# A fixed order for all five engines through attention, and the last batch's rows mixed with the first expert block

## The chip, the cores and the metric

The kernel runs on one core of a Trainium2 chip. The core has five engines that run at the same time and wait for one another through semaphores: PE (TensorE: matmuls, and transposes written as matmuls), DVE (VectorE), ACT (ScalarE), POOL (GpSimd) and SP (SyncE, which here only issues DMAs). The metric is the device time of one execution in microseconds; lower is better. The median of three runs of the kernel before is 874.22 us (874.01 to 875.73).

## The reference

Three stages follow one another. The first is attention with a decay bias over 4 batches and 8 heads of 576 positions of width 64; the second sends each of the 2304 rows of width 512 to one of 8 experts; the third is a dense feed-forward with a cosine.

```python
scores = scale * np.matmul(q, k.transpose(0, 1, 3, 2))
cum = np.cumsum(np.maximum(s, 0.0), axis=-1)
bias = -(cum[:, :, :, None] - cum[:, :, None, :])
scores = np.where(causal, -1e9, scores + np.minimum(bias, 0.0))
attn = np.exp(scores - np.max(scores, axis=-1, keepdims=True))
x = np.matmul(attn / (attn.sum(-1, keepdims=True) + 1e-09), v)   # rows of 512: 8 heads x 64
xn = x / (np.linalg.norm(x, axis=-1, keepdims=True) + 1e-06)
logits = xn @ en.T / tau                      # 8 experts
expert_idx = np.argmax(logits, axis=1)        # one expert each
out[mask] = gate_w[mask, None] * (np.maximum(x[mask] @ w1[e], 0.0) @ w2[e])
h = x @ w_in                                  # 2304 x 2048
y = (h * np.cos(h)) @ w_out
```

The norm of a row, its eight logits and its gate (the softmax value of the chosen expert) all need the finished row of attention, with all eight heads.

## The kernel before

**Attention** runs over 16 pairs of heads, four pairs for each batch. Of a pair, the scores of four groups of query tiles are made on PE (`s_ps`, `emit_s`), the decay bias is added and the row's extreme taken on DVE (L299), the exponential is on ACT (L565), PE turns the result around with 64-wide transposes into `t_ps` (L315), DVE and ACT copy these into `pt` and `pu` (L574, L571), and PE multiplies them with the values into `o_ps` (`av`, L340), which ACT and DVE copy into the batch's output `ot` (L645, L610). The loop runs this as a pipeline: in the turn of pair p stand the transposes and value products of pair p and the scores of pair p+1. In the trace the matmul `o_ps<-pt,v_t` with 320 columns comes once in each pair, so the distance between two of them is the time of one pair.

The decay bias of a pair comes from a tile `c_t`: SP loads it from a running sum that was written to memory at the start (`cumd`, L107, L109), and POOL adds the causal mask to it (`mask`, L129 to L134). `c_t`, q and k have two buffers each and are issued two pairs ahead, v has three. By the page a pair loads 320 KB of q, 496 KB of k, 320 KB of v and 800 KB of `c_t` (one DMA of 512 KB, two of 144), 1.98 MB in all. The zero fill of the expert buffer `xr` (eight DMAs of 768 KB, L250) is issued four at a time between the loads of two pairs.

**Rows.** When a batch's four pairs are done, a generator `rows(b)` is drawn forward a step at marked points of the loop (`point`). It makes the unnormalised logits with eight matmuls (`lp_ps`, L383), turns them (`lt_ps`, L404), turns the rows (`r_ps`, L361), scales them on DVE (L368), squares and sums them on ACT (L377), chooses the expert on DVE (L418 to L458), counts positions on PE (`rk_ps`), takes the square root of the squared norm with POOL's power and four DVE steps (`root`, L208 to L215), makes the gate, multiplies the rows with it (POOL L505 for the first three batches) and scatters them into `xr` (POOL L510). Logits, their transposes and the ranks use the two buffers of the score tile `s`. `rows(0)` does its first real work in pair 5; the rows of batch 2 therefore end after the loop, and those of batch 3 stand wholly behind it.

**Hand-over.** The largest expert after three batches is chosen (`pick_first`); 256 of its rows are loaded back from `xr` and turned (`early_rows`, `xe_ps` L549) into `the` and `tle`. The expert stage `moe1` walks through steps (r, f): r = -1 is the early block (256 rows, eight weight chunks), r = 0 is the rest of the same expert (128 rows), then seven more experts. A step is 12 matmuls `h_ps` (L867 to L869) and, one step later, 12 matmuls `acc` (L900 to L902), because each product is made of three parts (`wh`, `wl` are the upper and lower part of a weight chunk, split on ACT L802 and DVE L804). r = 0 starts with `xt_ps` (L835), the turned late rows, which need the scatter of the last batch.

Attention's SP, PE, ACT and DVE stand in program order; POOL there, and all but SP in `moe1`, are ordered by the framework's scheduler.

Of the kernel before, what the change touches and what calls it, by code (L numbers as in the profile page):

```python
# [41 lines left out]
@with_exitstack  # L42
def moe_kernel(ctx, tc, qd, kd, vd, sd, ied, embt, tau, ident, maskd, trid, wcat, wf, out):
    nc = tc.nc
    const = ctx.enter_context(tc.tile_pool(name="const", bufs=1))
    dram = ctx.enter_context(tc.tile_pool(name="dram", bufs=1, space=DRAM))
    xr = dram.tile([E * NT, DM], F32, name="xr")
    count = ctx.enter_context(tc.tile_pool(name="count", bufs=1))

    g = G()  # L50
    g.count = count
    early = ExitStack()
    ep = early.enter_context(tc.tile_pool(name="early", bufs=1, side="right"))
    g.the = ep.tile([128, 4, EARLY], F32R, name="the")
    g.tle = ep.tile([128, 4, EARLY], F32R, name="tle")
    g.tc, g.nc, g.const, g.dram, g.xr, g.out = tc, nc, const, dram, xr, out
    ET = mybir.EngineType
    with tc.manual_schedule(engines={ET.SP, ET.PE, ET.Activation, ET.DVE}):
        attention(g, qd, kd, vd, sd, ied, embt, tau, ident, maskd, trid)
    with tc.manual_schedule(engines={mybir.EngineType.SP}):  # L60
        st = ctx.enter_context(ExitStack())
        g.rawp = st.enter_context(tc.tile_pool(name="rawp", bufs=3, reuse_waits="tile"))
        g.ringp = st.enter_context(tc.tile_pool(name="ringp", bufs=RING, reuse_waits="tile"))
        g.x2p = st.enter_context(tc.tile_pool(name="x2p", bufs=1, reuse_waits="tile"))
        g.cv = st.enter_context(tc.tile_pool(name="cv", bufs=1, reuse_waits="tile"))
        g.chunks, g.tasks, g.loading = {}, [], {}
        moe1(g, wcat, wf)
# [11 lines left out]
def attention(g, qd, kd, vd, sd, ied, embt, tau, ident, maskd, trid):  # L79
    tc, nc, const, dram, xr = g.tc, g.nc, g.const, g.dram, g.xr  # L80
    with ExitStack() as st:
        ld = st.enter_context(tc.tile_pool(name="a_ld", bufs=2))
        one = st.enter_context(tc.tile_pool(name="a_one", bufs=1))
        sx = st.enter_context(tc.tile_pool(name="a_sx", bufs=8))
        otp = st.enter_context(tc.tile_pool(name="a_ot", bufs=2))
        sm = st.enter_context(tc.tile_pool(name="a_sm", bufs=4))
        xp = st.enter_context(tc.tile_pool(name="a_x", bufs=7))
        ps_s = st.enter_context(tc.tile_pool(name="ps_s", bufs=2, space=PSUM))
        ps_t = st.enter_context(tc.tile_pool(name="ps_t", bufs=4, space=PSUM))

        qt, kt, ct, vt = {}, {}, {}, {}
# [12 lines left out]
        def load_c(p):  # L104

            c_t = ct[p] = ld.tile([128, CT], F32, tag="c", name="c_t")
            nc.sync.dma_start(out=heads(c_t)[:, :, 128:640], in_=cumd[2 * p:2 * p + 2, 0:512].unsqueeze(0).to_broadcast([128, 2, 512]))  # L107
            for h in range(2):
                nc.sync.dma_start(out=c_t[64 * h:64 * h + 64, 2 * CH:CT], in_=cumd[2 * p + h].unsqueeze(0).to_broadcast([64, S]))  # L109

# [14 lines left out]
        def mask(p):  # L125

            c = heads(ct[p])
            tail = ct[p][:, CT - 64:CT]
            nc.gpsimd.tensor_tensor(out=tail, in0=tail, in1=mk_f[:, 128:192], op=ALU.add)  # L129
            mk = mk_f[:, 0:128].unsqueeze(1).to_broadcast([128, 2, 128])  # L130
# [5 lines left out]

        def load_v(p):
            vt[p] = ld.tile([128, 5, 128], F32, tag="v", name="v_t", bufs=3)
            nc.sync.dma_start(out=vt[p], in_=vd[p])
# [16 lines left out]
        ct[0] = ld.tile([128, CT], F32, tag="c", name="c_t")  # L156
# [3 lines left out]
        def first_c(k):  # L160
            sel = sel2 if k == 2 else idt[0:B * H, k:k + 1].to_broadcast([B * H, 128])
            for c0, eng in ((0, nc.scalar.copy), (288, nc.vector.tensor_copy)):
                ps = ps_t.tile([128, 512], F32, tag="t", name="c_ps")[:, 0:288]
# [4 lines left out]

        load(1)
        load_v(0)  # L170
        load_c(1)
        load_v(1)
        ie = one.tile([128, 256], F32, name="ie")
        lgs = one.tile([128, 640], F32, name="lgs")
# [7 lines left out]
        half5 = one.tile([128, 8], F32, name="half5")  # L182
# [7 lines left out]
        cacc = one.tile([128, E], BF16, name="cacc")  # L190
# [4 lines left out]
        prev = []  # L195

        def unordered(ins):

            for o in prev:
                tc.declare_no_dep(ins.ins, o, reason="rows that differ")  # L200
            prev.append(ins.ins)

        def root(out_t, in_t, w):

            a = sm.tile([128, 8], F32, tag="ra", name="ra", bufs=2)
            c = sm.tile([128, 8], F32, tag="rb", name="rb", bufs=2)
            y = sm.tile([128, 8], F32, tag="rc", name="rc", bufs=2)
            nc.vector.tensor_scalar(out=a[:, 0:w], in0=in_t, scalar1=1e-30, scalar2=None, op0=ALU.add)  # L208
            nc.gpsimd.tensor_tensor(out=y[:, 0:w], in0=a[:, 0:w], in1=half5[:, 0:w], op=ALU.pow)
            for _ in range(2):  # L210
                yield
            nc.vector.reciprocal(out=c[:, 0:w], in_=y[:, 0:w])
            nc.vector.tensor_tensor(out=c[:, 0:w], in0=c[:, 0:w], in1=a[:, 0:w], op=ALU.mult)
            nc.vector.tensor_tensor(out=c[:, 0:w], in0=c[:, 0:w], in1=y[:, 0:w], op=ALU.add)
            nc.vector.tensor_scalar(out=out_t, in0=c[:, 0:w], scalar1=0.5, scalar2=1e-6, op0=ALU.mult, op1=ALU.add)  # L215

        def setup():
# [4 lines left out]
            nc.gpsimd.memset(zr, 0.0)  # L222
            nc.gpsimd.memset(lgs[:, S:640], 0.0)
            nc.vector.memset(ones_f, 1.0)
            nc.vector.memset(half5, 0.5)
            nc.vector.memset(ones_b, 1.0)
            nc.vector.memset(cacc, 0.0)
            yield

            nc.gpsimd.iota(ei, pattern=[[1, E]], base=0, channel_multiplier=0)  # L230
            nc.vector.tensor_copy(out=ef, in_=ei)
            nc.vector.tensor_scalar(out=rev, in0=ef, scalar1=-1.0, scalar2=float(E), op0=ALU.mult, op1=ALU.add)
            nc.vector.tensor_scalar(out=eb, in0=ef, scalar1=float(NT), scalar2=None, op0=ALU.mult)
            for _ in range(8):
                yield
            nc.vector.tensor_copy(out=tri_b, in_=tri_f)
            nc.vector.tensor_tensor(out=sq, in0=emb_t, in1=emb_t, op=ALU.mult)
            yield
            yield "a"
            np_ = ps_s.tile([128, 2, 512], F32, tag="s", name="n_ps")[:, 0, 0:E]  # L240
            for kk in range(4):
                nc.tensor.matmul(out=np_, lhsT=ones_f, rhs=sq[:, kk, :], start=(kk == 0), stop=(kk == 3))
            yield "ra"
            yield from root(en, np_, E)
            nc.vector.tensor_scalar(out=en, in0=en, scalar1=tau_t, scalar2=None, op0=ALU.mult)
            nc.vector.reciprocal(out=ien, in_=en)
            for e in range(E):
                for _ in range(2):
                    yield
                nc.sync.dma_start(out=xr[e * NT:e * NT + 384].rearrange("(p c) d -> p c d", p=128), in_=zr.unsqueeze(1).to_broadcast([128, 3, DM]))  # L250

# [27 lines left out]
        def emit_x(n):  # L279
            p, tiles = steps[n]  # L280
            b, hp = divmod(p, H // 2)
            if b not in rs:
                rs[b] = sm.tile([128, 5, H], F32, tag="rs", name="rs", bufs=2)
                nc.gpsimd.memset(rs[b][:, 4, :], 1.0)
# [3 lines left out]
            for h in (2,) if tiles == (4,) else range(2):  # L288
                t = sx.tile([128, S], F32, tag="sx", name="s_sb")
                px[n].append(t)  # L290
                for i, (q0, q1), o in places(tiles):
                    mx = sm.tile([128, 1], F32, tag="mx", name="mx", bufs=20)
# [11 lines left out]
        def emit_t(n):  # L304
# [3 lines left out]
            tps = [ps_t.tile([128, 512], F32, tag="t", name="t_ps") for u in range(2)]  # L308
# [20 lines left out]
        def av(p, c0):  # L329
# [5 lines left out]
            o = ps_t.tile([128, 512], F32, tag="t", name="o_ps")  # L335
# [8 lines left out]
        def rows(b):  # L344
            s3 = [128, 5, E]
            o = ot.pop(b)
            ri = sm.tile([128, 5, H], F32, tag="ri", name="ri", bufs=2)
            ss = sm.tile([128, 5], F32, tag="ss", name="ss", bufs=2)
            l = small(s3, "l")
            order = list(range(5))[::-1] if b == B - 1 else list(range(5))  # L350
            xs, rr = {}, {}
            pick = choose(b, l)

            def turn(n):
                i = order[n]
                q0, q1 = QT[i]
                rr[i] = [ps_t.tile([128, 512], F32, tag="t", name="r_ps") for h in range(2)]
                for e in range(4):
                    for h in range(2):
                        hs = slice(64 * h, 64 * h + 64)  # L360
                        nc.tensor.transpose(rr[i][h][0:q1 - q0, 64 * e:64 * e + 64], o[hs, e, q0:q1], idt[hs, hs])  # L361

            def scaled(n):
                i = order[n]
                m = QT[i][1] - QT[i][0]
                x = xs[i] = xp.tile([128, DM], F32, tag="x", name="x")
                for h, r in enumerate(rr.pop(i)):
                    nc.vector.tensor_tensor(  # L368
                        out=x[0:m].rearrange("p (e c) -> p e c", e=4)[:, :, 64 * h:64 * h + 64],
# [854 lines left out]
```

## Time and profile before

| what | value |
|---|---|
| median of 3 runs | 874.22 us |
| profiled execution: its own time | 872.18 us |
| its span, first to last instruction | 870.4 us |
| PE busy | 810.1 us, 93% |
| DVE busy | 579.0 us, 67% |
| ACT busy | 428.1 us, 49% |
| POOL busy | 129.6 us, 15% |
| mean granted TensorE clock | 0.972 |

The page cuts the span into 40 equal slices and writes the busy share of each in tenths:

```profile
PE   7887989855999999999999999999999999999994
DVE  5765989846456565656589968775777748544462
PEclk9999999975999999999999999999999999999998
```

One digit is 21.8 us. A share of busy time mixes stages: here PE is full from slice 11 to the last but one, and has its holes in the first ten slices, which hold attention and the hand-over to the experts. The granted clock (last line) falls in slices 9 and 10.

### The profile page before, as it was taken

The numbers are of one execution on the slowest core, as the hardware profiler recorded it, in microseconds if no ns is written. First come the engines' busy times: TensorE is split into PE (matmuls) and PEld (weight loads), VectorE is DVE, ScalarE is ACT, GpSimd is POOL, SyncE is SP. The second block draws the span as 40 slices with busy tenths as digits, with TensorE's granted clock in tenths as the row PEclk, the third lists the DMA queues.
The fourth block names the chain that finished last, engine by engine and source line by source line (L and its number), as shares of the span: only waits on it lengthen the run. The fifth ranks groups of instructions, "written<-read, shape, count | busy, mean of one in ns | idle before, by whom it ended". The sixth has DMA issues, their size and how long they took to land. (4 is left out here: it accounts for less than half of the span.)

```text
span 870.4 us, 14996 instructions
## 1 busy us (share of the span) xinstructions
PE 810.1 (93%) x5534; PEld 672.2 (77%) x5534; DVE 579.0 (67%) x1323; ACT 428.1 (49%) x916; POOL 129.6 (15%) x183
## 2 busy tenths in 40 slices
PE   7887989855999999999999999999999999999994
PEld 3555656534999999999998888888888888888883
DVE  5765989846456565656589968775777748544462
ACT  4776878824354454555537545343444434333331
POOL 3413474542100111111000000000000000000132
PEclk9999999975999999999999999999999999999998
DMA  6997676305976767887543212110111100000122
GB/s 209 282 377 222 209 240 208 109 36 188 328 265 150 145 151 170 173 173 151 167 156 86 95 49 73 49 49 25 49 49 49 50 0 1 1 1 0 49 85 87
DMA packets 41228, 107.84 MB, mean 124 GB/s; under 512 B 7486, under 2 KB 7998, under 8 KB 41150
## 3 DMA queue, kind: packets, MB, share of 16 engines
q1 hardware_dynamic: 37550, 97.30, 38.9%
q0 software_dynamic: 3552, 9.45, 2.9%
q8 instruction: 45, 0.74, 0.4%
q14 instruction: 33, 0.27, 0.1%
q10 hardware_dynamic: 48, 0.07, 0.0%
HBM read 91.00 MB, written 15.81 MB: 123 GB/s over the span
## 5 line engine op out<-in xcount | busy, mean ns | idle before, releaser
L804 DVE TENSOR_TENSOR wl<-wraw,wh 128x1024 fp32r<-128x1024 f32 x64 | 78.4, 1225 | 76.7 <-ACT wh L802 71.4
L1120 PE MATMUL h_ps<-x2h,wh 128*128 128x512 f32 (+1 forms) x320 | 118.4, 371 | 0.0
L1122 PE MATMUL h_ps<-x2h,wl 128*128 128x512 f32 (+1 forms) x320 | 118.3, 370 | 0.0
L1121 PE MATMUL h_ps<-x2l,wh 128*128 128x512 f32 (+1 forms) x320 | 118.1, 370 | 0.0
L1140 PE MATMUL facc<-wh,gh 128*128 128x512 f32 x288 | 114.9, 399 | 1.3 <-ACT gh L1127 1.3
L1142 PE MATMUL facc<-wh,gl 128*128 128x512 f32 x288 | 113.8, 396 | 0.0
L1141 PE MATMUL facc<-wl,gh 128*128 128x512 f32 x288 | 113.8, 395 | 0.0
L981 ACT ACTIVATE ki<-h_ps 128x512 int32<-128x512 f32 (+1 forms) x80 | 44.6, 557 | 119.6 <-PE h_ps L1122 115.0
L982 DVE SCALAR_TENSOR_TENSOR ki<-ki,h_ps 128x512 f32<-128x512 int32 (+1 forms) x80 | 50.5, 632 | 71.3 <-ACT ki L981 68.2
L802 ACT CAST wh<-wraw 128x1024 fp32r<-128x1024 f32 x64 | 67.1, 1049 | 51.2 <-PE acc L901 44.3
L565 ACT ACTIVATE s_sb<-s_sb,mx 128x576 f32<-128x576 f32 (+2 forms) x144 | 82.8, 579 | 11.0 <-DVE mx L299 10.8
L1152 POOL DMA_INDIRECT out_dram<-oacc,ti x18 | 17.5, 971 | 435.0 <-DVE oacc L1150 431.4
L901 PE MATMUL acc<-hl,wh 128*128 128x256 f32 (+7 forms) x256 | 76.7, 301 | 0.9 <-DVE hl L873 0.8
L983 ACT ACTIVATE ki<-ki,hpi 128x512 f32<-128x512 f32 (+1 forms) x80 | 54.5, 682 | 46.9 <-DVE ki L982 46.2
L902 PE MATMUL acc<-hh,wl 128*128 128x256 f32 (+7 forms) x256 | 76.5, 300 | 0.0
L900 PE MATMUL acc<-hh,wh 128*128 128x256 f32 (+7 forms) x256 | 76.3, 304 | 0.0
L1127 ACT CAST gh<-ki 128x512 fp32r<-128x512 f32 (+1 forms) x80 | 46.2, 578 | 51.6 <-DVE ki L984 51.1
L1121 PEld LDWEIGHTS h_ps<-x2l,wh 128*128 128x128 f32 x320 | 60.1, 188 | 12.5 <-DVE x2l L908 0.6
L1120 PEld LDWEIGHTS h_ps<-x2h,wh 128*128 128x128 f32 x320 | 60.0, 188 | 12.2
L1122 PEld LDWEIGHTS h_ps<-x2h,wl 128*128 128x128 f32 x320 | 60.1, 188 | 11.1
L299 DVE CUSTOM_DVE_ANT_0 s_sb<-s_ps,c_t 128x512 f32<-128x512 f32 (+3 forms) x112 | 58.3, 542 | 15.3 <-POOL c_t L129 12.8
L867 PE MATMUL h_ps<-xth,wh 128*128 128x368 f32 (+6 forms) x224 | 68.2, 304 | 0.0
(220 smaller groups left out, 1709.4 us busy)
## 6 DMA issues: line engine op xcount, KB each, us to landing
wraw<-in_wcat_dram SPq DMA_DIRECT2D x64, 512.0 KB, 4.9
wraw<-in_wf_dram SPq DMA_DIRECT2D x32, 512.0 KB, 3.6
k_t<-in_kd_dram SPq DMA_DIRECT2D x16, 496.0 KB, 4.9
c_t<-cumd SPq DMA_DIRECT2D x15, 512.0 KB
xr<-zr SPq DMA_DIRECT2D x8, 768.0 KB, 11.3
q_t<-in_qd_dram SPq DMA_DIRECT2D x16, 320.0 KB
v_t<-in_vd_dram SPq DMA_DIRECT2D x16, 320.0 KB, 6.1
c_t<-cumd SPq DMA_DIRECT2D x30, 144.0 KB, 4.7
```

What stands on the lines that cost most here:

```text
L565: nc.scalar.activation(**kw)
L804: nc.vector.tensor_tensor(out=lo, in0=raw, in1=hi.bitcast(F32), op=ALU.subtract)
L867: nc.tensor.matmul(out=ps[:, 0:c], lhsT=wh[:, sl], rhs=th[:, k, 0:c], start=(k == 0), stop=False)
L900: nc.tensor.matmul(out=ps[:, 0:c], lhsT=wh[:, sl], rhs=hh[:, 0:c], start=(f == 0), stop=False)
L901: nc.tensor.matmul(out=ps[:, 0:c], lhsT=wh[:, sl], rhs=hl[:, 0:c], start=False, stop=False)
L902: nc.tensor.matmul(out=ps[:, 0:c], lhsT=wl[:, sl], rhs=hh[:, 0:c], start=False, stop=(f == 7))
L1120: nc.tensor.matmul(out=ps[:, 0:w], lhsT=wh[:, sl], rhs=g.x2h[:, k, a0:a1], start=(k == 0), stop=False)
L1121: nc.tensor.matmul(out=ps[:, 0:w], lhsT=wh[:, sl], rhs=g.x2l[:, k, a0:a1], start=False, stop=False)
L1122: nc.tensor.matmul(out=ps[:, 0:w], lhsT=wl[:, sl], rhs=g.x2h[:, k, a0:a1], start=False, stop=(k == 3))
L1140: nc.tensor.matmul(out=acc[t], lhsT=gh[:, sl], rhs=wh[:, 512:1024], start=(c == s), stop=False)
L1141: nc.tensor.matmul(out=acc[t], lhsT=gh[:, sl], rhs=wl[:, 512:1024], start=False, stop=False)
L1142: nc.tensor.matmul(out=acc[t], lhsT=gl[:, sl], rhs=wh[:, 512:1024], start=False, stop=(c == e))
```

## The change

Attention, the rows and the first seven steps of the expert stage are now one list, written out for all five engines, POOL included.

- **Rows** become a class whose steps are entered in a table of pair and place (`at(p, where, ...)`). Batch b starts in pair 4b+4, one pair earlier than before. The four outputs of a batch are squared on ACT as they finish (`squares`), and eight more matmuls of `lp` add up these squares, so that norm and logits come out of the same transposes. The square root is eight steps on POOL; for the first three batches the sum over heads and the positions also run on POOL. The rows are turned with full 128-wide transposes after the gate is known and are scaled once, by gate over sum (`rg`), straight out of PSUM.
- **Loads.** `c_t` has three buffers and is loaded three pairs ahead and masked earlier, v has two buffers, and the zero fill is spread over pairs 0 to 5. At the start `c_t` of pair 1 is loaded ahead of q, k and v.
- **Hand-over.** The first weight chunks are loaded in pair 14 and split in pair 15. `overlap` puts the rows of batch 3 between the steps of the early block.
- Pools are laid out anew, so that the weight buffers exist during attention; `lp`, `lt`, `rk` use the four buffers of the tile `t`.

```diff
+            for e0, src in enumerate((o, sqo)):
+                for k, ps in enumerate(self.p):
+                    for e in range(4):
+                        w = 256 if e0 else 128 + 32 * e
+                        nc.tensor.matmul(out=ps[32 * e:32 * e + 32, 0:288], lhsT=ie[:, w:w + 32], rhs=src[:, e, 288 * k:288 * k + 288],
+                                         start=not e0, stop=bool(e0))
...
-            c_t = ct[p] = ld.tile([128, CT], F32, tag="c", name="c_t")
+            c_t = ct[p] = ld.tile([128, CT], F32, tag="c", name="c_t", bufs=3)
...
+            at(p, "a", r.lp)
+            at(p, "ra", r.lcopy)
+            at(p, "b", r.lt)
+            at(p + 1, "rb", r.lw, r.choose, r.norm)
+            at(p + 1, "x0", r.choice)
+            at(p + 1, "a", r.rank)
+            at(p + 1, "ra", r.gate_a)
+            at(p + 1, "x3", r.gate_b, r.place)
+            at(p + 1, "b", r.gate_c)
...
+        at(15, "x0", early_load)
...
+        squares(NPAIR - 1)
+        r = g.r = Rows(B - 1)
+        r.lp()
+        r.lcopy()
+        early_rows()
+        r.lt()
+        r.lw()
+        r.choose()
+        r.choice()
+        r.norm()
...
+    h(0)
+    split_(3)
+    weigh(6)
+    h(1)
+    r.rank()
+    o(0)
+    r.gate_a()
+    r.gate_b()
+    r.place()
+    r.gate_c()
+    split_(4)
+    weigh(7)
+    h(2)
+    r.turn(4)
+    r.turn(3)
+    o(1)
+    r.scaled(4)
+    r.scaled(3)
...
+    r.turn(0)
+    o(4)
+    r.scaled(0)
+    s.raw32(9)
+    counts()
+    h(6)
+    o(5)
+    s.raw32(10)
+    s.x(0)
+    s.x(1)
```

PE from the last value product on, before: the whole chain of batch 3 (`lp`, `lt`, `r_ps`, `rk`) stands ahead of `xe_ps` and of the first expert matmul.

```order
L340 MATMUL o_ps<-pu,v_t 64x128 x2
...
L383 MATMUL lp_ps<-ot,ie 32x288 x8
L385 MATMUL lp_ps<-rs,ie 128x4
L361 MATMUL r_ps<-idt,ot 64x64 x8
L361 MATMUL r_ps<-idt,ot 128x64 x8
L404 MATMUL lt_ps<-idt,lgs 128x64 x10
L361 MATMUL r_ps<-idt,ot 128x64 x24
...
L549 MATMUL xe_ps<-idt,x 128x128 x8
...
L867 MATMUL h_ps<-the,wh 128x256
```

The same stretch of PE now, down to the first turned rows of batch 3:

```order
L379 MATMUL o_ps<-pu,v_t 64x128 x2
L407 MATMUL lp_ps<-ot,ie 32x288 x8
L407 MATMUL lp_ps<-sqo,ie 32x288 x8
L409 MATMUL lp_ps<-rs,ie 128x4
L574 MATMUL xe_ps<-idt,x 128x128 x8
L425 MATMUL lt_ps<-idt,lgs 128x64 x10
L936 MATMUL h_ps<-the,wh 128x256
...
L468 MATMUL rk_ps<-oh_all,tri_b 128x40
...
L515 MATMUL r_ps<-idt,ot 64x128 x4
L515 MATMUL r_ps<-idt,ot 128x128 x4
```

Moved: 24 matmuls `h_ps` stand between `lt` and the ranks, 12 `acc` and 12 `h_ps` between the ranks and the turned rows.

DMA queue of SP at the start, before (behind the loads of pair 0):

```order
L101 DMA q_t<-in_qd_dram 128x640
L102 DMA k_t<-in_kd_dram 128x992
L139 DMA v_t<-in_vd_dram 128x640
L107 DMA c_t<-cumd 128x2x512
L109 DMA c_t<-cumd 64x576 x2
```

The same place now, to the second `c_t`:

```order
L139 DMA c_t<-cumd 128x2x512
L141 DMA c_t<-cumd 64x576 x2
L133 DMA q_t<-in_qd_dram 128x640
L134 DMA k_t<-in_kd_dram 128x992
L145 DMA v_t<-in_vd_dram 128x640
L251 DMA ie<-in_ied_dram 128x288
```

The loads of pair 1 now stand behind `c_t`, which waits until the running sum has landed in memory.

POOL for the rows of a batch before, between two masks: one power, then multiplications and scatters.

```order
L209 TENSOR_TENSOR rc<-ra,half_138 128x5
L392 MEMSET ss 64x1
L131 TENSOR_TENSOR c_t<-c_t,mk_f 128x2x128
...
L505 TENSOR_TENSOR x<-x,gt 128x512 x2
L510 DMA xr<-x,pi 18432x512 x2
```

POOL for the rows of a batch now, as far as the power of the norm (the rest of the norm and the positions follow):

```order
L440 TENSOR_TENSOR lw<-lw,ri 128x40
L445 TENSOR_TENSOR lw<-lw 128x5x36
L445 TENSOR_TENSOR lw<-lw 128x5x18
L445 TENSOR_TENSOR lg<-lw 128x45
L446 TENSOR_TENSOR l<-lg,ien 128x40
L265 TENSOR_SCALAR ra<-lg 128x5
L266 TENSOR_TENSOR rz<-ra,half_142 128x5
```

The multiplications of whole rows have left POOL, and 13 small steps for the choice and the norm, then nine for the positions, have come to it.

## Rows read from the trace of the kernel before

**Rows 1.** Stretches: start:end, us, busy PE, PEld, DVE, ACT, POOL, PEclk, DMA share, GB/s
```profile
22.64:34.02 11.38, 9.01 (x112) 6.06 (x110) 7.96 (x30) 9.24 (x30) 3.89 (x7) 1.00 0.97 257
...
43.55:51.35 7.80, 7.68 (x104) 5.03 (x102) 6.48 (x26) 7.16 (x24) 0.00 (x0) 1.00 1.03 372
...
63.51:79.36 15.85, 11.14 (x130) 6.97 (x129) 6.75 (x24) 8.48 (x26) 5.44 (x9) 0.89 0.86 248
...
106.61:118.91 12.30, 9.78 (x130) 6.48 (x128) 9.85 (x37) 8.46 (x28) 10.03 (x13) 1.00 0.76 239
...
181.30:208.84 27.54, 9.19 (x87) 6.04 (x85) 12.44 (x53) 7.09 (x17) 12.36 (x12) 0.59 0.34 117
208.84:236.65 27.81, 26.59 (x193) 25.75 (x193) 17.77 (x50) 12.16 (x21) 5.31 (x6) 0.85 0.81 287
```

**Rows 2.** PE in order of time, hand-over: start, us, instruction, [idle before <-releaser]
```profile
180.54 0.82 PE L340 MATMUL o_ps<-pu,v_t 128*64 128x256 f32 x8
...
186.72 0.80 PE L404 MATMUL lt_ps<-idt,lgs 64*128 64x64 f32 x10 [2.79 <-ACT lgs L388]
...
202.91 0.45 PE L549 MATMUL xe_ps<-idt,x 128*128 128x128 f32 x1 [2.51 <-DMA x<-xr]
...
208.84 0.58 PE L867 MATMUL h_ps<-the,wh 128*128 128x256 f32 x1 [1.90 <-ACT wh L802]
...
237.98 2.05 PE L858 MATMUL h_ps<-x,w 128*128 128x128 f32 x16 [0.68 <-ACT x L836]
```

**Rows 3.** PE in order of time, two and two matmuls of the early block
```profile
211.90 0.42 PE L867 MATMUL h_ps<-the,wh 128*128 128x256 f32 x1
...
213.19 0.41 PE L867 MATMUL h_ps<-the,wh 128*128 128x256 f32 x1
...
217.87 0.28 PE L867 MATMUL h_ps<-the,wh 128*128 128x256 f32 x1
...
220.71 0.28 PE L867 MATMUL h_ps<-the,wh 128*128 128x256 f32 x1
```

**Rows 4.** Stretches of 1 us, for the granted clock
```profile
187.00:188.00 1.00, 0.52 (x10) 0.33 (x7) 0.47 (x2) 0.00 (x0) 1.00 (x2) 0.50 0.00 0
...
217.00:218.00 1.00, 1.00 (x11) 1.00 (x10) 1.00 (x2) 0.55 (x1) 0.88 (x1) 0.98 0.98 401
```

**Rows 5.** Waits, 22 to 64 us: who, for whom, us in total, times, longest
```profile
DVE s_sb L299 <- POOL c_t L129: 6.4, 2, 4.0
DVE rb L212 <- POOL rc L209: 2.5, 1, 2.5
...
POOL c_t L131 <- DMA c_t<-cumd: 26.2, 4, 13.2
```

**Rows 6.** Waits, 64 to 119 us
```profile
PE lp_ps L383 <- DVE mx L299: 1.5, 1, 1.5
...
DVE s_sb L299 <- POOL c_t L129: 6.0, 1, 6.0
```

**Rows 7.** Instructions in order of time, durations of single kinds (PE, DVE, ACT)
```profile
77.64 1.18 PE L383 MATMUL lp_ps<-ot,ie 128*32 128x288 f32 x16
...
236.65 0.66 PE L835 MATMUL xt_ps<-idt,xw 128*128 128x128 f32 x4
...
165.62 0.78 ACT L565 ACTIVATE s_sb<-s_sb,mx 128x576 f32<-128x576 f32 x1
...
166.05 0.69 DVE L299 CUSTOM_DVE_ANT_0 s_sb<-s_ps,c_t 128x512 f32<-128x512 f32 x1
...
169.41 0.55 DVE L410 TENSOR_TENSOR lw<-lt_ps,ri 128x160 f32<-128x160 f32 x2 [0.16 <-PE lt_ps L404]
```

**Rows 8.** Instructions in order of time, POOL and SP
```profile
102.54 1.18 POOL L209 TENSOR_TENSOR rc<-ra,half 128x5 f32<-128x5 f32 x1 [4.41 <-DVE ra L208]
...
197.31 0.93 POOL L510 DMA_INDIRECT xr<-x,pi  x1 [0.28 <-POOL x L505]
...
200.16 1.03 SPq L539 DMA_DIRECT2D x<-xr  x2
```

More of the change, by code (lines that the diff above doesn't have):

```diff
@@ L246, in setup, with setup_c, setup_d @@
+        def setup_c():
+            nc.vector.tensor_copy(out=en, in_=g.np)
+            root(en, en, E)
+            nc.gpsimd.tensor_scalar(out=en, in0=en, scalar1=tau_t, scalar2=None, op0=ALU.mult)
+        def setup_d():
             nc.vector.reciprocal(out=ien, in_=en)
[L247 to L250, printed above, removed]
@@ L342, in av, with squares @@
             return dict(out=ot[b][:, hp, c0:c1], in_=o[:, 0:c1 - c0])
[L344 to L355, printed above, removed]
+        def squares(p):
+            b, hp = divmod(p, H // 2)
+            nc.scalar.activation(out=sqo[:, hp, :], in_=ot[b][:, hp, :], func=ACTF.Square)
@@ L356, in turn @@
                 q0, q1 = QT[i]
-                rr[i] = [ps_t.tile([128, 512], F32, tag="t", name="r_ps") for h in range(2)]
+                r = self.r[i] = ps_s.tile([128, 2, 512], F32, tag="s", name="r_ps")[:, 0] if wide else g.bank("r_ps")
                 for e in range(4):
[L359 to L364, printed above, removed]
-                m = QT[i][1] - QT[i][0]
[L366 to L369, printed above, removed]
-                        in0=r[0:m, 0:256].rearrange("p (e d) -> p e d", e=4),
-                        in1=ri[0:m, i, h::2].unsqueeze(2).to_broadcast([m, 4, 64]), op=ALU.mult)
@@ L533, in pick_first, with load_first, early_load @@
             nc.vector.tensor_copy(out=pi, in_=pf)
[L534 to L536 removed]
+        def load_first():
+            g.first = nc.values_load(g.pi[0:1, 0:1], engines=(mybir.EngineType.SP,), min_val=0, max_val=E - 1)
+            g.expert = lambda r: g.first
+            g.raw = [weights(g, wcat, l) for l in range(3)]
+        def early_load():
+            g.xs = []
             for j in range(2):
@@ new lines, in weigh, with finish @@
+        def weigh(l):
+            raws[l] = weights(g, wcat, l)
+        def finish():
+            nonlocal x2h, x2l
+            x2h = g.x2h = g.x2p.tile([128, 4, SL], F32R, name="x2h")
+            x2l = g.x2l = g.x2p.tile([128, 4, SL], F32R, name="x2l")
+            for n in range(7, NS):
+                r, f = steps[n]
+                if n in load_at:
+                    l = load_at[n]
+                    if l < len(loads):
+                        load_w(l)
+                    else:
+                        start_chunk(g, wf, l - len(loads))
+                        advance(g.tasks)
+                emit_h(n)
```

626 lines of the change are left out of this document (330 added, 296 removed).

## Prediction

> **What bounds the kernel now.** I read the busy shares by slice first, then PE in order of time, then a table of stretches, then the waits of the stretches with holes. The slices say where time can be had: from 208.84 us on PE is the bound (26.59 of 27.81 us busy in the early block [rows 1]) and the change leaves the work behind that block as it is. So everything happens before the late rows' first product at 237.98 us [rows 2], and I cut this into two parts: attention up to the end of the last value product (180.54 + 0.82 = 181.4 us), and the hand-over from there to 237.98, 56.6 us.
>
> In attention a plain pair takes 7.80 us, of which PE works 7.68, while DVE has 6.48 and ACT 7.16 [rows 1]: PE is the bound of such a pair and DVE is close. Pairs are longer for two reasons. Early, PE waits for DVE, DVE for POOL's mask, and POOL for the load of `c_t`: DVE stood 6.4 and 6.0 us behind the mask, POOL 26.2 us behind the load [rows 5, 6]. The stretch 63.51 to 79.36 has only 11.14 us of PE in 15.85, at a clock of 0.89 [rows 1]. Later the rows of a batch stretch a pair to 12.30 us (PE 9.78, DVE 9.85), partly because `lp` must wait 1.5 us for a score buffer [rows 1, 6].
>
> In the hand-over PE works 9.19 of the first 27.54 us, at a mean clock of 0.59 [rows 1]. It waits for the logits' copy, for the scaled rows, for 256 rows read back from memory, and for the first weight chunk [rows 2]. Then the early block itself runs partly at half clock.
>
> The profiled execution took 872.18 us (span 870.4). The sums below are made against it; the median of the runs lies 2.0 us higher, which I add at the end.
>
> **The change, part by part: attention.** Start: the first value product stands at 22.64 [rows 1]. PE's order there is the same. `c_t` goes ahead of the next q and k, so these land later, but the running sum has less traffic ahead of it; I take 22.5, and 21 to 25 as ends.
>
> A plain pair stays at 7.7 to 7.8. The third buffer and the earlier mask put a whole pair between the landing of `c_t` and its use, so the waits of rows 5 and 6 on POOL go; late next would be q and k, still issued one pair ahead. Spreading the zero fill is free if the queue keeps up: in the plain pair the DMA share is already 1.03 at 372 GB/s, with 257 to 372 in the stretches around it [rows 1]. The loads of a pair are 1.98 MB, with a fill of 768 KB 2.77, with two 3.55; the six pairs with fills move 18.2 MB, 49 us at 372 GB/s and 71 at 257. The pairs themselves take 53 (8.3 + 8 + 8 + 10.7 + 9.6 + 8.6, below). I charge nothing, by the row nearest to such a load (372), and keep 18 us as the other end.
>
> Rows, per batch, on PE: `lp` is doubled, 2 x 1.18 = 2.4 us; five turns of four 128-wide transposes, by `xt_ps` (four in 0.66 with its tail) about 0.45 each, 2.3; `lt` and ranks 0.6 as before. Together 5.3 on top of 4 x 7.7 [rows 1, 7]. On DVE: two `lw` multiplications at 0.5; five scaled rows at 0.65 (a 512-wide operation that reads PSUM took 0.69); some 16 small steps at 0.2 [rows 7]. The square root's 2.5 us wait goes [rows 5], since its eight steps stand on POOL a pair ahead of their use. ACT loses five squares with their sums per batch and gains four 576-wide ones at 0.65 (the exponential of that width took 0.78 with its tail [rows 7]): 7.16 + 0.65 = 7.8 per pair, right at PE's time, so I count it as hidden but with no cover left.
>
> Which engine sets a pair: the one with `lp`, PE, 7.7 + 2.4 + 0.6 = 10.7; the next, DVE, 6.5 + 3.1 = 9.6 (`lw`, choice, reciprocals); the two with turns, PE, 8.6 each. That is 37.5 a batch. Before, four pairs with rows took 118.91 - 79.36 = 39.6. For the last three pairs of the loop I take 9.6, 10.5 (the choice of the first expert adds nine DVE steps) and 8.2. The sum: 22.5 + 8.3 + 8 + 8 (three pairs without rows) + 2 x 37.5 + 10.7 + 9.6 + 10.5 + 8.2 + 3.1 (last value product) = 163.9, and 0.4 for each of 15 hand-offs between engines that no row shows, 6: **170**. That is 11 us less. Most of it is the start: 22.64 to 79.36, 56.7 us now, becomes 44.6 and its share of the 6. Ends: PE alone, 22.5 + 15 x 7.7 + 3 x 5.3 + 3.1 = 157, a gain of 24; and a loss of 8, if the squares on ACT (16 x 0.65 = 10) lie open and little else goes.
>
> **The hand-over.** Times from the end T of the last value product. Copy of the output 0.6; 16 matmuls of `lp` 2.4 and the small one; eight transposes `xe` 1.0; two casts and two subtractions of 512 columns, of which the last ends 1.7 after the transposes: the first `h_ps` at T + 5.7. The read-back `x` has to be there: POOL's last scatter of batch 2 started at 197.31, SP issued the read at 200.16 and PE had the first half at 202.91 [rows 2, 8], 5.6 us; now three turned rows, their scaling and three scatters (0.93 each and as much again between two) take the first 6 us of the last pair, whose PE work is about 8, so the second half lands about 1 us late. T + 6.7. Two steps `h` take 2.84: 24 matmuls took 220.71 - 217.87 [rows 3]. DVE meanwhile makes `lw` and the choice, some 3.5 us, ahead of `hl`, so the ranks and the first `acc` come at T + 11. From there 13 groups of twelve at 1.42 to the end of step 6, five turns and ranks, 2.6: T + 32. Of `counts`, 21 small DVE steps of 0.2 stand before `hl` of step 6: 0.7 open. Group 7 and `xt` 2.1: T + 34.5. I add 1 for the late rows (their scatter ends 7 us of PE work ahead of `xt`, and needs the 5.6 us and DVE's and POOL's turn) and 1.7 for the clock. **T + 37.2**, against 56.6: 19.4 less.
>
> The clock: it stood at 0.50 at 187 us, after PE had waited 2.79 us, and was back at 0.98 at 217 us, after matmuls had run without a break since 211.9 [rows 2 to 4]. At half clock six matmuls took 1.29 us [rows 3], twelve 2.58. The new hand-over still has gaps of about 1 us around `lp`, `xe` and the choice. If the first four groups run at half clock they take 4 x 1.16 = 4.6 more, of which about 1 fills a gap that is there anyway; if none does, nothing. I take 1.7, nearer to the middle of 0 and 3.6 since these gaps are shorter than the 2.79 of the row. The Trainium skill, "TensorE: Matmul & The Clock Gate", Part 1, says that the throttled state is the default and that only sustained activity releases it. By that rule all four groups would be slow, and the sum T + 39. Ends for the hand-over: 29 (PE's own work only: `lp` 2.4, `xe` 1, `lt` 0.4, 16 groups 22.7, turns 2.6) and 44 (half clock to the end of step 2 and late rows that come 5 us late).
>
> Total: 872.18 - 11.4 - 19.4 = 841.4, and 2.0 for the runs: **843 us**.
>
> **Rivals.**
> 1. *The DMA queue takes the place of the mask.* q and k come late behind the fills and PE waits for them. For it: a DMA share of 0.97 and 1.03 in the two early stretches, and 257 GB/s in one of them [rows 1]. Against it: 372 in the other. Half-way, at 314 GB/s, the 18.2 MB take 58 us in place of 53, and one us more with the start: 849.
> 2. *The late rows gate the block.* `xt` now stands 7 us of PE work behind the last turned row, and its load queues behind six weight chunks of 512 KB. If it comes 6 us late: 849, with a hole ahead of `xt_ps` in PE's order. Against it: the chunks are issued as buffers come free, one pair per 3 us.
> 3. *PE becomes the bound nearly everywhere.* Attention ends near 162 and the hand-over takes 34: 832.
> 4. *Slower: POOL becomes the queue that all wait in.* Masks now stand behind small steps, and behind scatters that wait for DVE's scaled rows; DVE's choice waits for POOL's five-step chain, and PE for DVE. A power took 1.18 us on POOL [rows 8]. If every pair became as long as the worst with rows, 12.30: 22.5 + 15 x 12.3 + 3.1 = 210, 29 later than now, and with 19.4 gained behind it 884 on the runs. It decides from 11.7 us a pair on, where attention would end at 201. Against it: POOL was busy 3.89 us of 11.38 in an early stretch, and the row multiplications leave it (10.03 of 12.30 in the stretch that had them [rows 1]). The Trainium skill, "GPSIMD Engine Reference", Engine selection, gives element-wise work with two inputs to VectorE and calls GpSimd about twice as slow; it speaks for this rival, and no row here shows these small steps on POOL.
>
> **How the numbers follow.** Forecast (837 to 848) 0.5; rivals 1 and 2 together 0.25 (0.15 and 0.1); rival 3 0.19; rival 4 0.05; a mixture that cancels out 0.01. The range for 8 in 10 takes in rivals 1 to 3 and their bounds: 829 to 858. A change under 0.2% (1.7 us) can't be told from none in this kernel. Faster 0.94, same 0.01, slower 0.05.
>
> **What would show it.** In PE's order: value products 8 us apart in the first pairs, `xe_ps` and the first `h_ps` 5 to 8 us behind the last value product, and no wait of DVE for POOL's mask. Right in size if the first late product (the new line of L858) stands between 202 and 212 us. Wrong, if value products are over 10.4 us apart in the pairs without rows, if PE waits for q or k by more than 3 us in all, or if a wait of over 3 us stands before `xt_ps`. From there to the end the distance should stay at 632 us; if it changes by more than 2, work behind the block has been touched after all.

## The result, and the profile after

The changed kernel takes 850.36 us (median of 4, 849.89 to 854.12) where the kernel before, on the same chip, takes 874.98 (874.01 to 878.37): a ratio of 0.9721, 95% interval 0.9682 to 0.976. The forecast was 843 with a range of 829 to 858. So 24.6 us were gained where 31 were forecast. The profiled execution took 850.32 us, span 848.5, mean granted clock 0.985.

The stretches of the new trace that answer to [rows 1], each from one first value product to the next (a pair without rows, another, the second pair of a batch's rows, one with turns, the first pair of a batch's rows), then the hand-over. Columns: busy time of each engine, granted clock, DMA share, GB/s.

```profile
22.51:30.43 7.92, 7.68 (x105) 5.05 (x103) 6.50 (x26) 7.84 (x26) 3.07 (x5) 1.00 1.03 338
39.34:48.25 8.91, 7.75 (x104) 5.04 (x102) 7.67 (x30) 6.86 (x24) 5.64 (x14) 1.00 1.04 340
58.45:67.62 9.17, 8.53 (x120) 5.65 (x119) 7.48 (x30) 8.44 (x26) 7.03 (x16) 1.00 1.02 347
67.62:76.62 9.00, 8.85 (x110) 5.88 (x111) 8.86 (x36) 7.80 (x25) 5.39 (x18) 1.00 1.04 373
87.71:98.47 10.76, 10.64 (x142) 6.64 (x141) 7.86 (x25) 8.94 (x28) 7.16 (x12) 1.00 0.79 265
171.04:175.46 4.42, 4.42 (x52) 2.69 (x52) 2.42 (x6) 2.18 (x6) 0.00 (x0) 0.97 0.87 296
175.46:204.67 29.21, 25.27 (x213) 24.39 (x209) 21.34 (x62) 8.20 (x15) 12.37 (x24) 1.00 0.57 198
```

The pair that took 15.85 us is gone: the first five pairs together take 67.62 - 22.51 = 45.1 us, they took 56.7 (22.64 to 79.36). Between the last value product and the first expert matmul there are 4.4 us and not 27.5.

From 22 to 64 us DVE's two waits for POOL's mask, 6.4 us together [rows 5], have left the list; its first lines are now:

```profile
DVE ot L672 <- PE o_ps L379: 4.3, 4, 2.0
DVE rs L416 <- ACT lgs L415: 1.9, 1, 1.9
DVE ien L290 <- POOL en L287: 1.1, 1, 1.1
```

PE's hand-over in the order of time, answering to [rows 2] (start, duration, in brackets the idle time and what ended it):

```profile
165.44 4.32 PE L379 MATMUL o_ps<-pt,v_t 128*64 128x320 f32 x20 [0.89 <-ACT pt L596]
169.52 1.52 PE L379 MATMUL o_ps<-pu,v_t 128*64 128x256 f32 x8
173.99 1.09 PE L574 MATMUL xe_ps<-idt,x 128*128 128x128 f32 x8
175.46 0.39 PE L936 MATMUL h_ps<-the,wh 128*128 128x256 f32 x1
204.67 0.63 PE L904 MATMUL xt_ps<-idt,xw 128*128 128x128 f32 x4 [2.56 <-DMA xw<-xr]
206.16 1.05 PE L927 MATMUL h_ps<-x,w 128*128 128x128 f32 x4
```

Attention ends at 171.0 (forecast 170), the first late product stands at 206.16, 35.1 later (forecast 37.2). It stood at 237.98, so 31.8 us were gained up to here, 30.8 were forecast. But from here to the end of the span it is now 848.5 - 206.16 = 642.3 us and not 632.4. **The two forecast terms came out within 1.1 and 2.1 us, and 9.9 us were given back behind them.** About 2 of these go within the late block, where a half-clock stretch follows the wait of 2.56 us. The copies of each expert's result (`x2h`) then stand 29.3 to 30.0 us earlier than before for all experts, up to 424.58 against 454.31. The other 8 us go at the border to the third stage, in code that the change leaves alone. The waits of PE from 400 to 470 us, after (before, the list of the same place has only the 0.8 us for `hl`):

```profile
PE facc L1265 <- ACT gh L1252: 3.8, 1, 3.8
PE h_ps L1245 <- DVE x2l L977: 1.1, 1, 1.1
PE acc L970 <- DVE hl L942: 0.8, 1, 0.8
```

Followed back, `gh` waits for the first `ki` on DVE, and this stands behind the conversion of weights. In the kernel before the first `ki` on DVE starts at 460.02, 5.3 us after the first matmul of the stage (454.74), in the middle of a half-chunk's conversion:

```profile
459.42 0.68 DVE L1063 TENSOR_TENSOR cva<-cva,wh 128x512 f32<-128x512 f32 x1
460.02 0.68 DVE L982 SCALAR_TENSOR_TENSOR ki<-ki,h_ps 128x512 f32<-128x512 int32 x1
460.62 0.68 DVE L1064 TENSOR_TENSOR wl<-cva,cvp 128x512 fp32r<-128x512 f32 x1
```

After, it starts at 434.80, 8.6 us after the first matmul (426.21), and the whole next half-chunk (six steps from 431.14 on) has gone ahead of it. ACT stands in the same order: its cast for that half-chunk waits 3.30 us and goes ahead of its own first `ki`. DVE, then ACT:

```profile
433.40 0.68 DVE L1188 TENSOR_TENSOR cva<-cva,wh 128x512 f32<-128x512 f32 x1
434.19 0.69 DVE L1189 TENSOR_TENSOR wl<-cva,cvp 128x512 fp32r<-128x512 f32 x1
434.80 0.68 DVE L1107 SCALAR_TENSOR_TENSOR ki<-ki,h_ps 128x512 f32<-128x512 int32 x1
...
432.32 0.62 ACT L1186 CAST wh<-cva 128x512 fp32r<-128x512 f32 x1 [3.30 <-DVE cva L1095]
432.85 0.59 ACT L1106 ACTIVATE ki<-h_ps 128x512 int32<-128x512 f32 x1
```

The source of this stage is the same in both kernels. The framework's scheduler orders it, and it has set five half-chunks (but for the last step of the fifth) ahead of the first `ki` before, six after. Behind the wait PE also runs at a lower clock, 0.60 in the mean from 438 to 446 us.

### The profile page after: what moved, and what is told of

Same layout as the page of the kernel before. It is cut to its first block, busy times and chain, and to the rows that moved or that the text cites. A ratio compares the mean times of both kernels' runs of the same rounds, so it can differ in the third digit from the quotient of the medians.

```text
span 848.5 us, 14953 instructions
## 1 busy us (share of the span) xinstructions
PE 811.0 (96%) x5518; PEld 672.3 (79%) x5518; DVE 569.3 (67%) x1250; ACT 421.2 (50%) x894; POOL 138.3 (16%) x275
## 5 line engine op out<-in xcount | busy, mean ns | idle before, releaser
L1109 DVE TENSOR_TENSOR ki<-h_ps,ki 128x512 f32<-128x512 f32 (+1 forms) x80 | 50.7, 634 | 27.3 <-ACT ki L1108 25.7
L1265 PEld LDWEIGHTS facc<-wh,gh 128*128 128x128 f32 x288 | 54.6, 190 | 17.8 <-ACT gh L1252 6.4
```

The source lines that it names most:

```text
L1265: nc.tensor.matmul(out=acc[t], lhsT=gh[:, sl], rhs=wh[:, 512:1024], start=(c == s), stop=False)
```

## Experiments

The experiments ran on four chips. On three of them the kernel before takes 869 to 870 us, on that of the last run 875.2. **The changed kernel was run again on one of the three, called the second chip here,** together with three of the edits (the edge in the kernel before, the load of the late rows, the mixing undone):

> The changed kernel once more, unaltered, on the chip and in the same calls as the next three, so that they can be compared with it and not only with the kernel before. Both theories: a ratio of 0.972 to the kernel before, as first measured; some 846 us where the kernel before takes 870.

Measured: 847.18 us, ratio 0.9751 (0.9723 to 0.9779); span 844.4. Attention ends at 164.2 there, the first late product stands at 203.7. The profile of the kernel before with one edge (below, same speed as the kernel before) gives the other side on this chip: 179.3, 236.2 and a span of 867.2. Gained: 15.1 in attention, 32.5 at the first late product, 30.6 at the last `x2h` (452.62 to 422.06), 22.8 at the end. So the 8 us are given back at the border here too. Differences in us are against 847.2. For the runs on the other chips the ratio to the kernel before on the same chip is the safer measure: 0.9751 for the changed kernel.

**The border.** `h_cos_h` returns the `ki` instruction as well:

```diff
-            emit_h(n)
-            advance(g.tasks)
+            ins = emit_h(n)
+            if n < 1:
+                with tc.issue_after(ins.ins):
+                    advance(g.tasks)
+            else:
+                advance(g.tasks)
```

> One edge is added to the changed kernel: on VectorE, the conversion steps of the third stage's weights that are issued right after its first step stand behind the first step's ki operation. In the order the first ki then stands behind five converted half-chunks, as in the kernel before, not behind six. Theory (8 us of the gain are given back because one more half-chunk, some 4 us of VectorE, stands ahead of the first ki): 843 us, 7 less than the changed kernel, and the waits of the first value product of that stage for gh, 5.1 us now, fall to about 1.3. Rival (the loss is the clock or the weights' transfers and the order only shows it): 850, no change, and the wait only moves by a step.

Measured: 839.41 us, ratio 0.9653 (0.9627 to 0.968), 7.8 less, or 8.5 by the ratios. PE's wait for `gh` isn't in the list any more:

```profile
PE h_ps L1245 <- DVE x2l L977: 1.1, 1, 1.1
PE acc L970 <- DVE hl L942: 0.7, 1, 0.7
```

The first `ki` starts at 428.76, and the next half-chunk goes on behind it:

```profile
428.76 0.69 DVE L1107 SCALAR_TENSOR_TENSOR ki<-ki,h_ps 128x512 f32<-128x512 int32 x1 [0.40 <-ACT ki L1106]
429.36 0.69 DVE L1188 TENSOR_TENSOR cva<-cva,wh 128x512 f32<-128x512 f32 x1
```

The same edge in the kernel before:

> The edge of the first experiment is put into the kernel before, where the first ki stands behind five converted half-chunks already. Theory (the edge undoes what the changed kernel gave back, a sixth half-chunk): the kernel before gains only its own wait for gh, 1 to 2 us, ratio 0.998. Rival (the edge is an improvement of its own, and the changed kernel gave nothing back there): 6 us, ratio 0.993, as in the changed kernel.

Measured: 868.65 us, ratio 0.9998 (0.9977 to 1.002). The edge gives nothing where five half-chunks stand ahead anyway. So it is no improvement of its own; it puts back what the changed kernel lost. The theory holds in both directions. The wait for `gh` is 3.8 to 4.1 us in all nine runs of the changed kernel's kind without the edge and not in the list of the three that have it. Why the scheduler's order came out differently was not tried.

**The late rows.** First the scatter was moved ahead:

```diff
-    split_(4)
-    weigh(7)
     h(2)
...
     r.scaled(3)
+    split_(4)
+    weigh(7)
     split_(5)
...
     r.turn(1)
+    r.turn(0)
     o(3)
     r.scaled(1)
+    r.scaled(0)
...
-    r.turn(0)
     o(4)
-    r.scaled(0)
```

> The last turned tile of batch 3 is turned and scaled one step earlier, and the first two scaled tiles stand ahead of the split of chunk 4 on VectorE. Theory (the wait of 2.56 us ahead of xt_ps is the scatter chain on GpSimd, and the half clock of 205 to 208.7 us follows from that wait): the last scatter starts 2 us earlier, the wait falls below 1 us, the clock stays up, 847 to 848 us. Rival (the load's own way, from the last scatter's landing, sets it and the chain of scatters is bound by GpSimd): wait 1.5 us or more, 849 to 850.

Measured: 844.88 us, ratio 0.9716 (0.9686 to 0.9747), not told apart from the changed kernel; the wait ahead of `xt_ps` was 4.27 us (3.9 in the changed kernel on the second chip). The theory fell: the last scatter now starts 25.6 us after attention's end, 26.8 in the changed kernel, but the load that needs it is issued at 199.86, 9.0 us behind the scatter's start. So the load was moved in SP's order (with the edge above, this edit and the one below):

```diff
+    s.x(0)
     s.raw32(9)
     counts()
...
     s.raw32(10)
-    s.x(0)
     s.x(1)
```

> The kernel with the three edits, and the load of the late rows stands on SyncE's queue ahead of the last two pairs of weight chunks. Theory (the scatters of the late rows land 6 to 9 us after they start since they share the transfer engines with six chunks of 512 KB; with four of these issued behind the load, they land sooner): the wait ahead of xt_ps falls from about 3.7 to below 1.5 us, the first late product comes 2 to 4 us earlier, and the time is 3 us below the kernel with three edits, ratio 0.961 to 0.962. Rival (the time of a scatter is its own): the wait stays above 3 us, and the late weights come late on top: ratio 0.965 or above.

POOL's last scatter and SP's issues in the changed kernel on this chip, then in this one (`w` is a weight chunk, `xw` the late rows):

```profile
191.00 0.97 POOL L523 DMA_INDIRECT xr<-x,pi  x1 [1.37 <-DVE x L520]
191.02 0.92 SPq L872 DMA_DIRECT2D w<-in_wcat_dram  x2
198.89 0.34 SPq L884 DMA_DIRECT2D xw<-xr  x1
```

```profile
190.54 0.97 POOL L523 DMA_INDIRECT xr<-x,pi  x1 [0.19 <-issue]
193.75 0.35 SPq L884 DMA_DIRECT2D xw<-xr  x1
194.32 2.03 SPq L872 DMA_DIRECT2D w<-in_wcat_dram  x4
```

SP's load waits for the scatter in both. The scatter's landing is seen 3.2 us after its start and not 7.9: it had shared the transfer engines with the chunks. In the run with the three edits, where this load alone stands otherwise, it takes 8.5, and in all ten runs with six chunks ahead 6.3 to 9.0. The waits of PE from 180 to 215 us here:

```profile
PE xt_ps L914 <- DVE xtl L916: 3.6, 1, 3.6
PE xt_ps L904 <- DMA xw<-xr: 0.2, 1, 0.2
```

The wait ahead of `xt_ps` is gone and the first late product stands at 197.82, 5.9 us earlier than in the changed kernel (0.9 of this since attention ends earlier). But a wait of 3.6 us stands before the turned rows of the next expert. Followed back, it is ACT, which holds their cast behind the cast of a weight chunk that is still to be loaded, at a DMA share of 1.03 from 200 to 210 us:

```profile
210.43 1.04 ACT L98 CAST wh<-wraw 128x1024 fp32r<-128x1024 f32 x1 [3.52 <-DMA wraw<-in_wcat_dram]
```

The time is 839.11, ratio 0.9659 (0.9637 to 0.9681), that of the edge alone. Half of the theory holds (the wait), half fell (the time): the wait has moved to the next load on the full queue.

**POOL's queue in attention.** In the first profile the pair from 76.62 to 87.71 takes 11.09 us, where 8.6 were forecast. ACT waits 3.35 us in it. The profile names no releaser here (in four other runs it names POOL's next memset), but POOL's memset of the row sums, which the exponential adds to, ends just there (0.12 us at 85.69), behind a scatter, a mask and the mask's wait of 2.36 us for `c_t`:

```profile
85.84 0.78 ACT L590 ACTIVATE s_sb<-s_sb,mx 128x576 f32<-128x576 f32 x1 [3.35 <-issue]
```

```diff
-                nc.gpsimd.memset(rs[b][:, 4, :], 1.0)
+                nc.vector.memset(rs[b][:, 4, :], 1.0)
```

> The small memset that opens the row sums of a batch moves from GpSimd's queue to VectorE. Theory (in the pair from 76.62 to 87.71 us ScalarE's exponential waits 3.35 us for that memset, which stands on GpSimd behind a scatter, a mask and the late load of c_t): this interval falls from 11.09 to about 9.1 and the time by 2 to 848. Rival (that pair is held by the transfers): interval stays above 10.5 and the time at 850.

Measured: the interval is 9.09, as the theory had it; the time 845.29, ratio 0.9729 (0.9705 to 0.9753), 2 less in the medians but inside the intervals. On the second chip the changed kernel's own interval was 9.09 as well, so the time can't price the edit. The traces can show the link. With the memset on POOL the interval follows the mask's wait for `c_t`: 9.09 in both runs without a wait, 9.75 behind 1.25 us, 10.14 behind 1.65, 10.76 to 11.11 behind 2.25 to 2.36 (seven runs). With the memset on DVE it is 9.09 and 9.10 behind waits of 2.28 and 2.34. About 0.5 us comes back: the pair behind takes 11.22 in the three runs with the edit, 10.75 or 10.76 in five of the others. With the three edits:

> The three edits together. If their theories hold and add up: 7 + 2.5 + 2 less than 850.4, 839 us. If the third stage's order depends on more than the one edge, 843 to 848.

Measured: 840.31 us, ratio 0.9655 (0.9631 to 0.9679): the edge's gain, and nothing on top that can be told.

The other way round, the small steps were taken off POOL (in `choose`, `place` and `root`: `nc.vector` for `nc.gpsimd`, the power stays):

```diff
-                e = nc.vector if b == B - 1 else nc.gpsimd
+                e = nc.vector
```

> The small steps of the choice, the place and the norm's root (not the power) move from GpSimd to VectorE for the batches 0 to 2; for the last batch only the root's steps move. Theory (VectorE sets the second pair with rows, 9.17 us, and GpSimd's time there is free): VectorE gets 2.5 to 3 us more in that pair, which becomes 10.5 to 12, three times: 4 to 8 us slower. Rival (hand-offs between the two engines cost as much as the steps): within 2 us.

Measured: 864.16 us, ratio 0.994 (0.9921 to 0.996), 17 slower: the theory has the sign, but the time lost is twice its upper end. The pair after the first `lp` in this run, and PE's waits from 55 to 165 us:

```profile
58.28:71.89 13.61, 10.44 (x119) 6.85 (x119) 10.59 (x42) 8.37 (x25) 4.88 (x9) 0.79 0.98 343
```

```profile
PE s_ps L315 <- DVE mx L338: 10.6, 9, 3.2
```

DVE has 10.59 us of work in that pair in place of 7.48 (3.1 more, as expected), but the pair is 4.4 us longer: the extra steps stand in one piece ahead of the scores, PE waits for them and the clock falls to 0.79. The piece holds a wait as well, since the power stayed on POOL:

```profile
65.38 0.17 DVE L267 TENSOR_TENSOR rc<-ra,rz 128x5 f32<-128x5 f32 x1 [1.31 <-POOL rz L266]
```

So the run prices the steps on DVE together with this hand-off; with the power moved too, the loss was not measured.

**The start of attention.** The prefetch of `c_t` undone:

```diff
-            c_t = ct[p] = ld.tile([128, CT], F32, tag="c", name="c_t", bufs=3)
+            c_t = ct[p] = ld.tile([128, CT], F32, tag="c", name="c_t")
...
-                load_c(p + 3)
+                load_c(p + 2)
```

> The prefetch of c_t alone is undone: two buffers in place of three, the load two pairs ahead as before, and the mask on GpSimd ahead of the second group of value products of the pair before its use. Theory (of the 15 us that attention gained on this chip 11.4 lie in the first five pairs, and the waits of VectorE for the mask, 12.4 us in all before, went by the prefetch): the first five pairs, 46 us in the changed kernel, take 54 to 57 again and the time rises by 8 to 11 us. Rival (the waits went since GpSimd lost the row multiplications and the fills are spread): the first five pairs stay below 49 and the time rises by 2 us or less.

Measured: 847.28 us, ratio 0.9762 (0.9727 to 0.9797). The first five pairs take 45.6 us (46.1 in the changed kernel on the second chip). From 22 to 80 us DVE waits 2.9 us for the first part of the mask, where it was 12.4 in the kernel before. **The theory fell, and with it the cause in the prediction.** A new one came from SP's order in the kernel before: POOL's long waits for `c_t` follow the groups of four fills. So these were put back as well:

```diff
-        fills = [0, 1, 2, 3, 4, 4, 5, 5]
+        fills = [1, 1, 1, 1, 2, 2, 2, 2]
```

> On top of the undone prefetch (which alone changed nothing) the zero fills of 768 KB go back to two groups of four, in the second and the third pair. Theory now (the 13.3 and 11.3 us that GpSimd waited for c_t in the kernel before are the time of four fills ahead of it on the same transfer queue; spreading the fills, not the third buffer, took these waits away): GpSimd waits over 8 us for c_t once or twice again, the first five pairs take 51 to 57 us in place of 45.6, the time is 6 to 10 us above 847. Rival (the waits went because the first transfers and the setup loads stand earlier): the first five pairs stay below 48 and the time within 2 us of 847.

Measured on a chip where the kernel before takes 875.19: 863.51 us, ratio 0.9876 (0.9844 to 0.9908), 0.0114 above the run with only the prefetch undone, 10 us. The first five pairs take 55.2 (21.91 to 77.14), and DVE waits 11.6 us for that first part from 22 to 80 us. POOL's mask in the kernel before (with the edge) and in this run:

```profile
55.69 0.72 POOL L131 TENSOR_TENSOR c_t<-c_t,mk_f 128x256 f32<-128x256 f32 x1 [13.29 <-DMA c_t<-cumd]
```

```profile
61.34 0.32 POOL L176 TENSOR_TENSOR c_t<-c_t,mk_f 128x64 f32<-128x64 f32 x1 [11.38 <-DMA c_t<-cumd]
```

The new theory holds with two buffers. Whether four fills would do harm with three was not tried, so the third buffer may have been enough without the spread.

**The squares and the mixing.**

```diff
-            for e0, src in enumerate((o, sqo)):
+            for e0, src in enumerate((o,)):
...
-            nc.scalar.activation(out=sqo[:, hp, :], in_=ot[b][:, hp, :], func=ACTF.Square)
+            pass
```

> Left out: the squares on ScalarE and the second half of the logits' products on TensorE that sums them; the norm's root is taken of another positive 128x5 number, so the gates aren't the reference's. Theory (TensorE sets the pair that has the logits' products and ScalarE's squares are hidden): the three pairs of 10.2 to 10.8 us fall to about 9.5, the other pairs stay, and with the last batch the time falls by 4 to 5 us. Rival (ScalarE has no cover left, as its busy time of 8.4 in a pair of 9.17 suggests): the other pairs fall too, by 0.5 each, 8 to 12 us in all.

Measured: 841.78 us, ratio 0.9691 (0.9663 to 0.9718), 5.4 less, or 5.2 by the ratios. The three pairs with `lp` take 9.23, 9.78 and 9.78 in place of 10.20, 10.75 and 10.76; the pairs right behind them stay at 9.17 to 9.49. ACT's squares are hidden, the second half of `lp` on PE is not.

The mixing undone (rank, gates, five times `turn` and `scaled` ahead of `h(0)`, then the steps with nothing between):

```diff
+    r.rank()
...
+    r.turn(0)
+    r.scaled(0)
     h(0)
```

> The mixing alone is undone: all rows of batch 3 (ranks, gates, five turned and scaled tiles) stand ahead of the first expert's first step, as in the kernel before; everything else is as in the changed kernel. Theory (the mixing hides the chain choice, gates, scaled rows under products; in the changed trace this chain ends at about 188 us where the first product stood at 175.5): the first product comes 10 to 12 us later, the turned tiles are then no longer between the products (3 us back) and the wait ahead of xt_ps goes (2 to 4 back): 5 to 8 us slower than the changed kernel. Rival 1 (the mixing is nearly all of the 19.4 us that the hand-over gained): 17 us or more slower. Rival 2 (the late rows set the first late product in both orders): within 2 us of it.

Measured: 849.68 us, ratio 0.9769 (0.9745 to 0.9793), 2.5 slower in the medians and 3.6 in the spans, with overlapping intervals. PE now waits ahead of the ranks, and the first product stands 12.5 us later:

```profile
176.28 0.19 PE L468 MATMUL rk_ps<-oh_all,tri_b 128*128 128x40 bf16 x1 [4.32 <-DVE oh_all L459]
183.55 0.56 PE L936 MATMUL h_ps<-the,wh 128*128 128x256 f32 x1
```

The wait ahead of `xt_ps` is gone, so the first late product comes only 6.1 us later (209.81). Two more come back in the late block, where the clock stays at 1.00 (205 to 220 us); in the changed kernel it was 0.50 from 200 to 205 and 0.84 from 205 to 210. The theory has the steps; its 5 to 8 was a little too much. Rival 1 fell: without the mixing the way from attention's end to the late product is 45.2 us, with it 39.6, before it was 56.9. So the mixing is a third of what the hand-over gained. The rest came with the shorter chain of the rows, the early read-back and the weights split during attention; what each of these gave was not tried.

## Why the prediction was right, and where not

**Attention, right in size.** The pairs were forecast at 8.3, 8, 8, 10.7, 9.6, 8.6, 8.6, 10.7, 9.6; measured on the first chip 7.92, 8.91, 8.91, 10.20, 9.17, 9.00, 11.09, 10.76, 9.17. PE sets the pair with `lp`, as forecast; the run without squares shows it. In the pairs with turns PE is busy 8.85 us of 9.00, but DVE is as full (8.86). That DVE sets the pair behind `lp` the row doesn't show: DVE is busy 7.48 us of 9.17, PE 8.53. The sum without hand-offs is 163.9; on the first chip 7.1 us came on top, 2.5 of them in the pair of 11.09 and 3.8 from 155.91 on (9.53 and 5.6 where 8.2 and 3.1 were forecast: the last 20 matmuls take 4.32 us at half clock, the 20 of the pair before 2.28). On the second chip these pairs take 9.09 and 7.16, and attention ends at 164.2, the sum without hand-offs. So the 6 us for hand-offs are a term that no run shows, and that 170 came out on the first chip is luck: a wait and a stretch at half clock stood in its place.

**Attention, wrong in cause.** "The third buffer and the earlier mask put a whole pair between the landing of `c_t` and its use, so the waits of rows 5 and 6 on POOL go": DVE's waits on POOL went, but with two buffers and the late mask they go as well (12.4 us to 2.9) once the fills are spread, a term that I had at nothing. With the fills spread, the prefetch is worth nothing that can be measured. The other 4 us or so that attention gained on the second chip, behind the first five pairs, were not taken apart.

**Hand-over, right in sum.** First `h_ps` at T + 4.4 (6.7 forecast), first `acc` at T + 9.0 (11), first late product at T + 35.1 (37.2). The forecast sum has a slip: 32 + 0.7 + 2.1 is 34.8 and not 34.5. On the second chip the first `h_ps` stands at T + 6.9, behind a wait of 1.6 us for the read-back, and the first late product at T + 39.6: there the hand-over loses part of what attention gained. On the first chip the early block's first groups run at full clock (PEclk 1.00 from 175.46 on), so the 1.7 for the clock weren't due there; the clock was at half (0.50) from 165.44 to 169.76, behind waits of 1.43 and 0.89 us, during the last value product. The gaps ahead of the block that the term rested on weren't there: PE is busy all of the 4.42 us up to 175.46. So the four slow groups and T + 39 did not come. The rule of the Trainium skill, "TensorE: Matmul & The Clock Gate", Part 1, is that the throttled state is the default and activity releases it. This trace doesn't speak against that rule; what failed is how the prediction applied it.

**Rival 2, right in part.** The 1 us for late rows was 2.56, and 3.9 on the second chip, where it passes the 3 us that the prediction named as a sign of being wrong. Its reason was the one given (the chunks of 512 KB on the queue), but it acts on the scatter, not on the load behind it, and removing it moves the wait to the next expert.

**Rival 4, in small.** POOL's order makes the 11.09 pair 2 us longer; some 1.5 of them go with the memset on DVE, since 0.5 comes back in the pair behind. But its larger part was wrong: POOL's small steps cost less there than on DVE, by 17 us with the wait for the power.

**The step that failed:** "the change leaves the work behind that block as it is", and with it the distance of 632 us. It became 642.3, which the prediction's own sign (more than 2 us of change) calls work touched behind the block. Of the 9.9 us more, 7.8 are one half-chunk of conversion that the scheduler set ahead of the third stage's first step, and 2.1 are the late block. With the edge that puts it back, the ratio 0.9653 gives 844.6 us on the first chip's 874.98, against 843 forecast.

## What to carry to other kernels

Where a scheduler orders a stage, source that a change leaves alone is not work that it leaves alone: compare the instruction order behind the change too, above all where one stage's preparation stands ahead of the next stage's first step. Several edits that all could remove a wait share one forecast but not one cause; undo them one at a time and, where one alone changes nothing, two together. A large transfer ahead of a small urgent one is paid by whoever waits for the small one: spread the large ones, and expect the wait to move when the queue is full anyway.

## What the runs showed of the hardware

The same small step (`l<-lg,ien`, 128x40) takes 0.264 us on POOL (3 times) and 0.201 on DVE. By their starts, the root's 128x5 steps behind the power follow one another at 0.28 us on POOL (changed kernel) and at 0.20 on DVE (the run with the steps moved). The Trainium skill, "GPSIMD Engine Reference", Engine selection, calls GpSimd about twice as slow for two inputs; at these sizes the traces show 1.3 and 1.4 times.

A scatter of 128 rows had landed, as seen by SP's next load, 3.2 us after its start with two chunks `w` of 512 KB issued ahead of that load (one run) and 6.3 to 9.0 us with six (ten runs).

Behind two waits of PE in the changed kernel's first profile a stretch at a lower mean clock followed: 0.66 from 205 to 210 us behind the wait of 2.56, 0.60 from 438 to 446 behind that of 3.8. Part of what these waits cost is paid after them.
